# Linear attention and a mixture of adapters: numerators in four quarters of the array, slots in pairs of half-heads, no arithmetic on GpSimd

## The chip, the cores and the metric

The kernel runs on one core of a Trainium2 chip. The metric is device time in microseconds, the median of the runs given. Its engines are TensorE (PE, with the weight loads listed apart as PEld), VectorE (DVE), ScalarE (ACT), GpSimd (POOL) and SyncE (SP); each works through its own queue in order.

## What is computed

Two stages in a row. `B = H = 8`, sequence 576, head dimension 64; 4608 tokens of 512 features; 8 adapters of rank 16.

```python
q_p = phi(q, cos_w, sin_w)           # concat(relu(q)*cos(pos), relu(q)*sin(pos)): 128 features
k_p = phi(k, cos_w, sin_w)
kv  = einsum('bhsf,bhsd->bhfd', k_p, v)
z   = sum(k_p, axis=2)
num = einsum('bhsf,bhfd->bhsd', q_p, kv)
den = einsum('bhsf,bhf->bhs', q_p, z)[..., None] + 1e-06
x   = (num / den), heads side by side             # (4608, 512)
logits = x @ w_gate                               # 8 adapters, top 2, softmax over the two
out = x + sum over the two of weight * (x @ A[e]) @ B[e]
```

## The kernel before

**Tiling.** The batches go in four pairs `P` = 0 to 3 (batches 2P and 2P+1). A token index is `9*p + j`, so partition `p` (64 of them per batch) holds nine *slots* `j`; a slot of a pair is 128 tokens, one partition each. Heads come as four head pairs per batch, `2a + hh` with `a`, `hh` in 0, 1 (each head pair `c` has its two heads on the two halves of the partitions, `par`).

**Loads** (`load`, L437 and L439). K, V and Q of a batch are read as float32 and written as bfloat16 by DMAs that GpSimd issues, in halves (`a` = 0, then 1) for P = 0 and whole for P = 1 to 3: 12 half loads (288 KB written) and 18 whole ones (576 KB). The planner lets at most eight be in flight; a ninth waits for the first to land.

**KV stage of a batch.** `relu_k` (L446 on ACT, L448 on DVE or GpSimd) clips K in place. `vscale` makes VV, V scaled by cos and by sin of the position, one instruction per half on DVE (L464), nine per half, one for each slot, on ACT (L462) or on GpSimd (L458). `kv_mm` (L474) makes 72 products per batch, contraction 64, output 64 x 130, in 64 x 64 quarters of the array. `kv_evac` copies the sum from PSUM into BD, a block-diagonal tile (two heads on the diagonal, the rest zero, cleared once by `c_bd`, L364): two copies of 64 partitions for each KV result (L495 on ACT, L497 on DVE).

**A step of a slot.** `qt_mm` (L548) transposes Q by TensorE; `qt_evac` (L555, ACT) clips it into `qTcs[:,0]`; `qt_tan` (L562, DVE) multiplies by a table of tangents into `qTcs[:,1]` (the sine part is the cosine part times the tangent; the cosine cancels between numerator and denominator); `num_mm` (L574) forms 16 products of contraction 128, 64 columns of weights, 130 moving columns, against BD; `x_rden` (L587) and `x_xt` (L593) divide on DVE. P = 0 does a slot in two steps, one for each `a`; P = 1 to 3 in one.

**The adapters of two or three slots.** `xt_mm` (L603) transposes x, `xt_evac` copies it (a helper `copy`, L609 on ACT, L611 on DVE); `za_mm` (L622) multiplies by the adapters' A and the gate; `r_max`, `r_mask`, `r_sig`, `r_zg` (L637 to L661) choose the top two and weight them; `zg_mm` (L670) transposes; `dx_mm` (L681, L683) adds x and the adapters' B product; `osb` copies to SBUF; `store` (L694) is a DMA that SP issues. There are 13 such groups.

**Set-up.** `c_tan_mm` and `c_tan` make the table of tangents. `c_s4` fills S4, four shifted selections of the identity, on GpSimd (a memset, L352, and four copies, L354); `w_turn` (L403, L407) permutes A and the gate with it into AW, which every `za` needs.

**The order.** Nothing is ordered by hand in the text. Every step is given to a `Planner` with a duration, its needs, the buffers it uses and a due time; two long lists, `PLACES` (due times) and `CHOICE` (which of a step's engines), fix the outcome. The planner plays the steps through and the instructions are emitted in the order it finds, so each engine's queue, GpSimd's and SP's too, has a fixed order.

Of the kernel before, what the change touches and what calls it, by code (L numbers as in the profile page):

```python
# [14 lines left out]
ALU = mybir.AluOpType  # L15
# [4 lines left out]
LATENCY = {"PE": 0.22, "DVE": 0.15, "ACT": 0.18, "POOL": 0.2, "SP": 0.0}  # L20
DMA_RATE = 0.4e6
DMA_LATENCY = 1.4
# [6 lines left out]
    -101.8, -87.98, -82.42, -89.88, -75.22, -41.37, -75.2, -69.56, -114.61, -12.34, -86.45, -23.58, -23.54, -91.8,  # L29
    -45.05, -82.9, -23.77, -85.62, -30.55, -18.3, -22.53, -9.1, -38.95, -15.08, -65.11, -79.01, -56.96, -87.63,  # L30
    -56.28, 33.12, -45.48, 14.06, 72.95, -105.45, -131.87, -86.42, -70.75, -32.34, -16.92, -63.84, -25.14, -17,
    -43.98, -53.84, -48.45, -28.91, -9.38, -65.93, 17.22, -37.67, -38.2, -56.96, -43.01, -39.86, 30.02, 5.68, -111.22,
    -41.2, -64.86, -27.22, -29.22, -28.93, -4.21, -45.87, 23.7, -11.07, -12.97, 6.07, 70.31, -15.27, -0.79, 4.41,
    27.35, 80.46, 18.33, 55.75, -26.51, 7, 9.96, 5.54, 33.89, 26.46, 7.17, 53.85, -11.53, 34.73, 17.11, 14.52, 31.08,
    37.76, -22.01, -12.04, 32.65, -13.69, 63.75, 37.46, 47.44, 56.06, 90.6, -13.41, 25.03, 66.69, 7.86, 110.2, 48.71,
    70.14, 38.66, 102.11, 76.76, 2.02, 55.03, 13.27, 84.09, 49.59, -19.61, -52.1, -38.03, -36.37, -69.95, 12.85,
    -59.13, -37.48, -46.73, -48.82, -56.02, 13.89, 12.78, 15.65, -74.65, -22.83, -80.13, -60.11, 3.79, -21.31, -7.57,
    1.52, 3.72, -39.7, 0.51, 12.71, 28.08, -19.88, -4.04, 3.48, -28.4, -22.6, -107.17, -85.77, 16.75, 13.19, -35.9,
    -0.64, -30.78, 17.84, 81.24, 31.53, -2.77, 44.36, 65.3, 56.03, -1.94, 1.8, 32.86, 13.11, 4.12, 78.55, -26.18,
    28.07, 38.04, -31.26, 7.2, -32.61, -33.96, 31.37, -48.1, 23.76, 25.15, 68.01, 27.37, -44.65, 11.78, 45.25, 16.38,  # L40
    46.68, -22.64, 13.69, -25.72, -66.73, -0.53, -0.78, 71.43, 51.94, -23.6, -20.35, 24.46, 19.13, -1.34, 82.95,
    76.08, 23.7, -17.43, 12.4, -67.27, -50.55, -14.11, -46.79, 3.18, 15.81, -42.31, 39.03, 34.99, -39.11, 9.69, -18.7,
    -1.38, -56.98, 11.6, 73.43, 36.89, 10.81, 42.1, 9.54, -35.43, 6.89, 52.15, -23.59, 26.68, -12.27, 11.85, -7.33,
    25.43, -12.89, 48.12, -20.49, -5.27, -64.21, -51.87, 23.84, -27.03, -119.07, 63.64, 75.64, 28.22, -21.9, 39.45,
    76.49, 37.89, -23.87, 71.2, 66.21, 4.08, 64.69, 89.26, 43.11, 2.03, 58.06, 26.58, 65.92, 39.82, 30.03, 43.53,
    40.19, 71.59, 24.18, 64.92, 67.13, 22.92, -33.78, 25.67, 15.63, -6.52, 35.07, 11.11, 13.68, -24.37, 35.57, -39.99,
    -14.59, 78.65, -60.34, 46.82, 2.41, 16.29, -84.28, 12.65, -18.86, -31.15, -1.35, -75.63, -16.46, -81.15, -29.57,
    27.98, 47.97, 84.51, 85.87, 41.03, 66.04, 24.09, 50.35, -11.39, 79.39, 17.42, -26.65, 48.38, 31.89, 37.07, 11.76,
    19.75, -22.61, 31.8, -62.39, -30.12, -16.33, 78.09, 5.97, 40.99, 27.88, 53.62, 10.42, 32.04, 86.77, 43.98, 44.81,
    115.53, 53.53, 36.54, 45.14, 38.01, 72.24, 6.57, 97.39, 34.2, 67, -3.53, 18.47, 37.85, 94.56, 45.82, -9.21, 49.09,  # L50
    -29.83, -18.99, 63.72, -55.17, -7.86, 29.25, 43.71, 38.01, 53.05, 60.43, 30.63, 34.35, 40, 87.14, 3.29, 77.97, 52,
    51.6, 50.13, 10.4, 17.19, 59.75, 47.81, 17.21, 87.08, 61.73, 63.61, 93.31, 21.46, 55.47, 28.59, 31.38, -29.79,
    66.6, 49.37, -5.21, 0.73, 95.14, 89.51, 37.48, 19.5, 12.15, 80.24, 34.55, 53.72, 64.45, 4.15, 11.76, 57.62, 8.52,
    50.43, -6.44, -11.99, -14.41, -2.71, -20.63, 64.98, 69.49, 62.23, 41.36, -24.4, 64.99, -57.64, 32.08, 0.58, 0.18,
    -51.16, -19.52, -12.18, 37.93, 44.64, 53.74, 38.51, 16.7, 67.44, 60.26, 35.36, 55.27, 13.68, 23.18, -7.26, 30.35,
    2.86, 6.2, 51.01, 5.37, 37.66, 77.13, 79.47, 91.93, 14.78, 78.89, 35.85, 48.44, -3.31, -44.41, 67.02, 30.92,
    32.02, 42.36, -16.67, 44.14, 76.86, 65.68, -57.2, 42.99, 0.26, 95.71, -7.34, 49.33, 18.77, 68.25, 41.77, 57.26,
    73.06, 46.33, 58.36, 11.34, 119.4, 45.36, 152.93, -7.4, 79.07, 58.86, 28.26, 43.32, -37.77, 97.2, 15.02, 59.13,
    18.9, 55.86, 87.03, 74.35, 17.63, 89.53, 45.25, 75.81, -29.62, 68.21, 101.01, 86.91, 62, 92.26, 30.42, 20.38,
    89.46, 57.05, 38.98, 84.93, 88.33, 73.29, 10.34, 0.12, 86.89, 62.77, 41.35, 67.7, 72.99, 79.09, 20.79, 16.54,  # L60
    10.7, 23.33, 87.48, 88.63, 56.65, 13.55, 13.26, 70.38, 29.36, 90.47, 83.93, 74.51, 109.97, 81.76, 144.25, 15.07,
    68.55, 46.86, 113.6, 170.36, 66.36, 23.82, -21.97, 83.74, 94.21, 71.03, 89.76, 55.2, 84.29, 58.94, 49.33, 57.55,
    43.72, 58.13, 58.8, 75.42, 44.54, 72.47, 46.3, 17.6, 45.55, 112.71, 61.5, 49.18, 85.32, 91.99, 65.9, 49.76,
    102.45, 64.06, 109.11, 80.81, 98.13, 79.93, 109.32, 109.38, 106.64, 12.94, 78.35, 68.82, 51.61, 126.26, 51.11,
    48.51, 64.21, 89.64, 100.47, 96.74, 26.02, 67.7, 101.32, 95.25, 20.01, 35.48, 76.22, 70.63, 64.08, 8.78, 62.96,
    124.43, 72.7, 125.02, 67.06, 106.24, 98.77, 100.23, 116.59, 171.53, 99, 30.9, 96.57, 105.21, 70.96, 125.86, 61.23,
    98.87, 56.59, 37.62, 27.7, 95.05, 100.15, -77.12, 31.54, 170.49, 49.8, 58.28, 113.97, 78.54, 91.49, -30.01,
    113.81, 85.19, 124.99, 154.41, 102.88, 93.56, 84.87, 90.61, 132.83, 145.49, 116.13, 61.55, 20.49, 107.23, 74.22,
    92.66, 68.29, 175.11, 55.65, 161.84, 136.23, 34.27, 108.62, 44.45, 91.08,
]  # L70
CHOICE = [
    0, 0, 0, 0, 0, 0, 0, 0, 0, 0, 0, 0, 0, 0, 0, 0, 0, 0, 0, 0, 0, 0, 0, 0, 0, 0, 0, 0, 1, 0, 0, 1, 0, 0, 0, 0, 0, 0,
    1, 0, 1, 1, 0, 0, 0, 1, 0, 1, 0, 1, 1, 0, 0, 0, 1, 0, 0, 0, 0, 0, 0, 0, 0, 0, 1, 0, 0, 0, 1, 0, 0, 0, 0, 0, 2, 0,
    0, 0, 0, 0, 0, 1, 0, 1, 0, 0, 1, 0, 0, 0, 2, 0, 0, 0, 0, 0, 0, 0, 0, 0, 0, 1, 0, 0, 1, 0, 0, 0, 2, 0, 0, 0, 1, 0,
    0, 0, 0, 0, 0, 0, 0, 0, 0, 0, 0, 0, 0, 0, 0, 0, 0, 0, 0, 0, 0, 0, 0, 0, 0, 0, 0, 0, 0, 0, 0, 0, 0, 0, 0, 0, 0, 0,
    0, 0, 0, 1, 0, 0, 0, 0, 0, 0, 1, 0, 0, 0, 0, 0, 1, 0, 0, 0, 0, 0, 0, 0, 0, 0, 0, 0, 0, 0, 0, 0, 0, 0, 0, 0, 0, 0,
    0, 0, 0, 0, 0, 0, 0, 1, 0, 0, 0, 0, 0, 0, 0, 0, 0, 0, 0, 0, 0, 0, 0, 0, 0, 0, 0, 0, 0, 0, 0, 0, 1, 0, 0, 0, 0, 0,
    0, 0, 0, 0, 0, 0, 0, 0, 0, 0, 0, 1, 0, 0, 0, 0, 0, 0, 0, 0, 0, 0, 0, 0, 0, 0, 0, 0, 0, 0, 0, 0, 0, 0, 0, 0, 0, 0,
    0, 1, 0, 0, 0, 0, 0, 0, 0, 0, 0, 0, 0, 0, 0, 0, 0, 0, 0, 0, 0, 0, 0, 0, 0, 0, 0, 0, 0, 0, 0, 0, 0, 0, 0, 0, 0, 0,
    0, 0, 0, 0, 0, 0, 0, 0, 0, 0, 0, 0, 0, 0, 0, 0, 0, 0, 0, 0, 0, 0, 0, 0, 0, 0, 0, 0, 0, 0, 0, 0, 0, 0, 0, 0, 0, 0,  # L80
    0, 1, 0, 0, 0, 0, 0, 0, 0, 0, 0, 0, 0, 0, 0, 0, 0, 0, 0, 0, 0, 0, 0, 0, 0, 0, 0, 0, 0, 0, 0, 0, 0, 0, 0, 0, 0, 0,
    0, 0, 0, 0, 0, 0, 0, 0, 0, 0, 1, 0, 1, 0, 0, 0, 0, 0, 0, 0, 0, 0, 0, 0, 0, 0, 0, 0, 0, 0, 0, 0, 0, 0, 0, 0, 0, 0,
    0, 1, 0, 0, 0, 0, 0, 0, 1, 0, 0, 0, 0, 0, 0, 0, 0, 0, 0, 0, 0, 0, 0, 0, 0, 0, 0, 0, 0, 0, 0, 1, 0, 0, 0, 0, 0, 0,
    0, 0, 0, 0, 0, 0, 0, 0, 0, 0, 0, 0, 0, 0, 1, 0, 0, 0, 0, 0, 0, 0, 0, 0, 0, 0, 0, 0, 0, 0, 0, 0, 0, 0, 0, 0, 0, 0,
    0, 0, 0, 0, 0, 0, 0, 0, 0, 0, 0, 0, 0, 0, 0, 0, 0, 0, 0, 0, 0, 0, 0, 0, 0, 0, 0, 0, 0, 0, 0, 1, 0, 0, 0, 0, 0, 0,
    0, 1, 0, 0, 0, 0, 0, 0, 0, 0, 0, 0, 0, 0, 0, 0, 0, 0, 0, 0, 0, 0, 0, 0, 0, 0, 0, 0, 0, 0, 0, 0, 0, 0, 0, 0, 0, 0,
    0, 0, 0, 0, 0, 0, 0, 0, 1, 0, 1, 0, 0, 0, 0, 0, 0, 0, 0, 0, 0, 0, 0, 0, 0, 0, 0, 0, 0, 0, 0, 0, 0, 0, 0, 0, 0, 0,
    1, 0, 0, 1, 1, 0, 0, 0, 1, 0, 0, 0, 0, 0, 0, 0, 0, 1, 0, 0, 0, 0, 0, 0, 1, 0, 0, 1, 1, 0,
]

# [128 lines left out]
def kernel(  # L222
# [16 lines left out]
    ER = E * R  # L239
    AW_W = ER + E  # L240
    J = 9
    NP = S // J
    assert NP == 64 and H == 8 and D == 64 and B == 8 and DM == 512 and ER == 128
    W = D + 1
    VW = 2 * (D + 2)
    HALF_B = 128 * 2 * J * D * 4
    ALL = range(4)

    persist = ctx.enter_context(tc.tile_pool(name="persist", bufs=1))
    psum = ctx.enter_context(tc.tile_pool(name="psum", bufs=1, space=bass.MemoryType.PSUM))  # L250

# [99 lines left out]
    def c_s4():  # L351
        nc.gpsimd.memset(S4, 0.0)  # L352
        for i in range(4):
            nc.gpsimd.tensor_copy(S4[:, i].rearrange("p (q f) -> p q f", f=4)[:, :, i], ident)  # L354
# [455 lines left out]
```

## Time and profile before

| | |
|---|---|
| median of 8 runs | 131.61 us (130.78 to 132.88) |
| the profiled execution's own time | 132.88 us |
| its span, first to last instruction | 131.1 us |
| mean granted TensorE clock | 0.91 |
| DVE busy | 108.84 us in 300 instructions |
| PE busy, PE weight loads | 96.24 us, 72.39 us |
| ACT busy | 88.15 us in 200 instructions |
| POOL busy | 51.78 us in 57 instructions |
| DMA bytes | 24.14 MB: 14.43 MB by the loads' queue, 9.44 MB by the stores' |

The span is 1.8 us shorter than the time of its own execution and 0.5 us below the median. "Busy" counts the time in which an engine has at least one instruction at work; two neighbours on DVE can overlap by about 0.1 us, so durations sum to more than busy time. A matmul's end is modelled and has some 0.2 us of pipeline in it, so eight matmuls of 0.22 us each take far less than eight times that. In the rows by slices, a digit is the busy share of 1/40 of the span (3.28 us) in tenths.

### The profile page before, as it was taken

Reading aid. Unit: us, or ns where it says so; the run is one execution under the profiler, and the core shown is the slowest. Engines: PE = TensorE matmul, PEld = TensorE weight load, DVE = VectorE, ACT = ScalarE, POOL = GpSimd, SP = SyncE. Lnnn points to the kernel's source line nnn. Section 1 sums busy time; section 2 is a strip of 40 time slices with the busy share of each in tenths; the row PEclk is TensorE's granted clock in tenths of the full one; section 3 lists DMA queues with packets and bytes.
Section 4 is the critical chain, followed back from the end, with each engine's and each line's share of the span. In section 5 each row is a group of like instructions: output and inputs, shape, how many; then the busy total and the mean of one; then the engine's idle time right before and its main releaser. Section 6 shows DMA issues by size and latency. Waiting matters only on the chain.

```text
span 131.1 us, 4453 instructions
## 1 busy us (share of the span) xinstructions
PE 96.2 (73%) x1860; PEld 72.4 (55%) x1872; DVE 108.8 (83%) x300; ACT 88.2 (67%) x200; POOL 51.8 (39%) x57
## 2 busy tenths in 40 slices
PE   0153494896999874863999995367989999999830
PEld 0122482795876363723886772256866768786400
DVE  6634798789979894999889799999999899998940
ACT  3954699569963897990647797177544887877440
POOL 6996984228429999399000059300000000000000
PEclk9999998559999999996589999778699999999995
DMA  1999999999999999999999999900000655005583
GB/s 12 157 148 205 207 207 205 208 192 208 210 206 209 207 324 324 210 208 207 208 208 324 209 237 295 294 26 7 0 5 2 243 242 241 4 12 232 240 345 138
DMA packets 15989, 24.14 MB, mean 184 GB/s; under 512 B 1889, under 2 KB 14305, under 8 KB 15969
## 3 DMA queue, kind: packets, MB, share of 16 engines
q0 software_dynamic: 14096, 14.43, 66.5%
q1 hardware_dynamic: 1872, 9.44, 17.9%
q8 instruction: 14, 0.23, 0.7%
q14 instruction: 7, 0.05, 0.1%
HBM read 28.85 MB, written 9.44 MB: 292 GB/s over the span
## 4 chain that ended last, share of the span: by engine, by line
PE 32%; DVE 31%; ACT 12%; POOL 9%; issue 6%; DMA 6%; POOLq 0%; DVEq 0%; ACTq 0%
DVE qTcs L562 9%; PE pnd L574 9%; ACT VV L462 7%; POOL VV L458 7%; DVE xt L593 6%; PE pnd L474 6%; DMA Kr<-in_k_dram 6%; PE ps L622 5%; PE ps L603 4%; PE ps L548 4%; DVE zg L661 3%; PE ps L681 2%; DVE rden L587 2%; DVE osb L611 2%; DVE m L637 2%
## 5 line engine op out<-in xcount | busy, mean ns | idle before, releaser
L574 PE MATMUL pnd<-BD,qTcs 128*64 128x130 bf16 x576 | 28.7, 244 | 8.6 <-DVE qTcs L562 3.3
L574 PEld LDWEIGHTS <-qTcs 128*64 128x64 bf16 x576 | 22.0, 122 | 13.7 <-issue 6.8
L593 DVE TENSOR_TENSOR xt<-pnd,rden 128x512 bf16<-128x512 f32 (+1 forms) x45 | 25.8, 582 | 1.1
L562 DVE TENSOR_TENSOR qTcs<-qTcs,TT 128x512 bf16<-128x512 bf16 (+1 forms) x45 | 25.9, 598 | 0.4 <-ACT qTcs L555 0.2
L555 ACT ACTIVATE qTcs<-ps 128x512 bf16<-128x512 bf16 (+1 forms) x45 | 21.4, 511 | 5.2 <-PE ps L548 4.7
L609 ACT COPY xT<-ps 128x512 bf16<-128x512 bf16 x26 | 15.1, 583 | 13.7 <-PE ps L603 13.7
L462 ACT ACTIVATE VV<-Vb,TVf 128x128 bf16<-128x128 bf16 (+1 forms) x54 | 19.3, 443 | 3.7 <-DMA Vb<-in_v_dram 3.7
L448 POOL TENSOR_SCALAR Kr<-Kr 128x2304 bf16<-128x2304 bf16 x2 | 12.5, 6244 | 16.6 <-DMA Kr<-in_k_dram 16.6
L609 ACT COPY osb<-ps 128x512 f32<-128x512 f32 (+1 forms) x31 | 16.5, 561 | 3.3 <-PE ps L683 1.6
L474 PE MATMUL pnd<-VV,Kr 64*64 64x130 bf16 x576 | 13.5, 256 | 7.0 <-DVE Kr L448 3.1
L603 PE MATMUL ps<-ident,xt 128*128 128x128 bf16 x144 | 14.1, 228 | 6.1 <-DVE xt L593 5.5
L474 PEld LDWEIGHTS <-Kr 64*64 64x64 bf16 x576 | 11.7, 131 | 8.6 <-DVE Kr L448 3.4
L464 DVE TENSOR_TENSOR VV<-Vb,TV 128x2304 bf16<-128x2304 bf16 (+1 forms) x13 | 14.6, 1143 | 1.2 <-DMA Vb<-in_v_dram 1.2
L548 PE MATMUL ps<-ident,Qb 128*64 128x128 bf16 x288 | 15.0, 247 | 0.1
L603 PEld LDWEIGHTS <-xt 128*128 128x128 bf16 x144 | 9.2, 100 | 10.2 <-DVE xt L593 6.8
L681 PE MATMUL ps<-xt,ident 128*128 128x512 bf16 x34 | 13.0, 382 | 0.6 <-DVE osb L611 0.3
L548 PEld LDWEIGHTS <-Qb 128*64 128x64 bf16 x288 | 11.3, 128 | 3.0 <-issue 1.8
L622 PE MATMUL ps<-AW,xT 128*128 128x136 bf16 x144 | 11.6, 234 | 0.1
L458 POOL TENSOR_SCALAR VV<-Vb,TVf 128x256 bf16<-128x256 bf16 x9 | 10.1, 1132 | 2.2 <-DVE xT L611 2.2
L622 PEld LDWEIGHTS <-xT 128*128 128x128 bf16 x144 | 9.8, 103 | 1.2 <-issue 0.2
L683 PE MATMUL ps<-Ball,zgT 128*128 128x512 bf16 x26 | 9.9, 380 | 0.6 <-DVE zgT L611 0.3
L495 ACT CAST BD<-pnd 64x520 bf16<-64x520 f32 (+1 forms) x11 | 5.9, 538 | 4.9 <-PE pnd L474 3.9
(62 smaller groups left out, 119.4 us busy)
## 6 DMA issues: line engine op xcount, KB each, us to landing
out_dram<-osb SPq DMA_DIRECT2D x11, 768.0 KB, 4.4
Kr<-in_k_dram POOLq DMA_DIRECT2D x6, 576.0 KB, 19.3
Vb<-in_v_dram POOLq DMA_DIRECT2D x6, 576.0 KB, 16.3
Qb<-in_q_dram POOLq DMA_DIRECT2D x6, 576.0 KB, 21.9
Vb<-in_v_dram POOLq DMA_DIRECT2D x4, 288.0 KB, 8.1
Kr<-in_k_dram POOLq DMA_DIRECT2D x4, 288.0 KB, 8.1
Qb<-in_q_dram POOLq DMA_DIRECT2D x4, 288.0 KB, 9.2
out_dram<-osb SPq DMA_DIRECT2D x1, 512.0 KB, 3.3
```

Source lines behind the costliest of these rows:

```text
L458: nc.gpsimd.tensor_scalar(out=o[:, :, j], in0=i[:, :, j], scalar1=TVf[:, cs, j:j + 1], scalar2=None, op0=ALU.mult)
L462: nc.scalar.activation(o[:, :, j], i[:, :, j], AF.Copy, scale=TVf[:, cs, j:j + 1])
L474: nc.tensor.matmul(out=pt[64 * hh:64 * hh + 64, par, a * 2 * W:(a + 1) * 2 * W], lhsT=kt[64 * par:64 * par + 64, 2 * a + hh, j, :], rhs=vt ...
L548: nc.tensor.transpose(out=pt[64 * hh:64 * hh + 64, o:o + 128], in_=qt[:, 2 * a + hh, j, :], identity=ident)
L555: nc.scalar.activation(tQT[S_(uqt)][:, 0, 0:n].rearrange("p g s -> p (g s)"), pB(up)[:, 0:n * 64], AF.Relu)
L562: nc.vector.tensor_tensor(out=t[:, 1, 0:n], in0=t[:, 0, 0:n], in1=TT[:, j].unsqueeze(1).to_broadcast([128, n, NP]), op=ALU.mult)
L574: nc.tensor.matmul(out=nd[64 * b2:64 * b2 + 64, a, 0:4 * W].rearrange("p (h e w) -> p h e w", h=2, e=2)[:, :, par], lhsT=qt[:, cs, (b2 * l ...
L593: nc.vector.tensor_tensor(out=tXT[S_(uxt)].rearrange("p (a h d) -> p a h d", a=2, h=4)[:, aa[0]:aa[-1] + 1], in0=nd_view(und, aa)[:, :, :, ...
L603: nc.tensor.transpose(out=pB(up)[:, c * 128:(c + 1) * 128], in_=tXT[S_(uxt)][:, c * 128:(c + 1) * 128], identity=ident)
L609: nc.scalar.copy(o, i)
L622: nc.tensor.matmul(out=pF(uza)[:, n * AW_W:(n + 1) * AW_W], lhsT=tXTT[S_(u)][:, c, :], rhs=AW[:, c, :], start=(c == 0), stop=(c == 3))
L681: nc.tensor.matmul(out=pF(udx), lhsT=ident, rhs=tXT[S_(uxt)], start=True, stop=False)
```

## The change

1. `num_mm` no longer uses a block-diagonal tile. `kv_evac` is one copy of 128 partitions into a plain tile KVs; each numerator product is cut in two, contraction 64 and 65 moving columns: 32 products a step where there were 16, in the four quarters of the array (two row halves `hh`, two column halves `b2`), each row half with a PSUM bank of its own. The tile BD and its four memsets go.
2. P = 0 and P = 1 (`SPLIT`) form steps of two neighbouring slots and one `a`, instead of (P = 0) one slot and one `a` or (P = 1) one slot and both. P = 1's K, V and Q are loaded in halves too: 24 half loads and 12 whole ones. The tile xt now holds two slots; there are 11 of them (before, 12 of one slot).
3. GpSimd's alternatives for `relu_k` and `vscale` are removed. In the order before, GpSimd did two whole relu's of K and one whole half of VV. GpSimd keeps the loads and the set-up.
4. `c_s4` is a memset and one `affine_select` of 128 x 2048. The tangent and weight set-ups are cut into parts that each hold one PSUM bank.
5. The planner's constants and durations are changed a little and both lists are new, so the order on every engine is another.

```diff
-        nc.gpsimd.memset(S4, 0.0)
-        for i in range(4):
-            nc.gpsimd.tensor_copy(S4[:, i].rearrange("p (q f) -> p q f", f=4)[:, :, i], ident)
+        nc.gpsimd.memset(S4, 0.0)
+        nc.gpsimd.affine_select(out=S4, in_=S4, compare_op=ALU.not_equal, fill=1.0, base=0,
+                                pattern=[[1, 4], [-1, DM]], channel_multiplier=4)
...
-                (nc.gpsimd if eng == "POOL" else nc.vector).tensor_scalar(out=t, in0=t, scalar1=0.0, scalar2=None, op0=ALU.max)
+                nc.vector.tensor_scalar(out=t, in0=t, scalar1=0.0, scalar2=None, op0=ALU.max)
...
-            if eng == "POOL":
-                for j in range(J):
-                    nc.gpsimd.tensor_scalar(out=o[:, :, j], in0=i[:, :, j], scalar1=TVf[:, cs, j:j + 1],
-                                            scalar2=None, op0=ALU.mult)
-            elif eng == "ACT":
+            if eng == "ACT":
...
-    def kv_evac(hh, aa, up, ubd, eng):
-            o = tBD[S_(ubd)][64 * hh:64 * hh + 64, :, lo:lo + n, :, 66 * hh:66 * hh + W]
-            i = pND[S_(up)][64 * hh:64 * hh + 64, :, lo * 2 * W:(lo + n) * 2 * W]
+    def kv_evac(aa, up, ukv, eng):
+            o = tKV[S_(ukv)][:, :, lo:lo + n, 0:W]
+            i = pND[S_(up)][:, :, lo * W:(lo + n) * W].rearrange("p e (x w) -> p e x w", w=W)
...
-                        for b2 in range(2):
-                            bd = tBD[S_(("BD", 2 * P + b2))]
-                            nc.tensor.matmul(
-                                out=nd[64 * b2:64 * b2 + 64, a, 0:4 * W].rearrange(
-                                    "p (h e w) -> p h e w", h=2, e=2)[:, :, par],
-                                lhsT=qt[:, cs, (b2 * len(aa) + n) * 2 + par, :],
-                                rhs=bd[:, par, a, cs].rearrange("p (h w) -> p h w", h=2)[:, :, 0:W],
-                                start=(cs == 0), stop=(cs == 1), skip_group_check=True)
+                        for hh in range(2):
+                            for b2 in range(2):
+                                kv = tKV[S_(("KV", 2 * P + b2))]
+                                nc.tensor.matmul(
+                                    out=nd[64 * b2:64 * b2 + 64, hh, (2 * x + par) * W:(2 * x + par + 1) * W],
+                                    lhsT=qt[64 * hh:64 * hh + 64, cs, ((jj * 2 + b2) * na + n) * 2 + par, :],
+                                    rhs=kv[64 * hh:64 * hh + 64, par, 2 * aa[n] + cs, 0:W],
+                                    start=(cs == 0), stop=(cs == 1), skip_group_check=True)
...
+        if P in SPLIT:
+            parts = [(js, [a]) for a in range(2) for js in ([0, 1], [2, 3], [4, 5], [6, 7], [8])]
+        else:
+            parts = [([j], [0, 1]) for j in range(J)]
```

The instruction counts that follow from the two orders, with the shapes of the profile:

| | before | after |
|---|---|---|
| PE num products | 576 of 128 x 64, 130 columns | 1152 of 64 x 64, 65 columns |
| DVE tangent, reciprocal, xt | 27 full + 18 half each | 34 full + 4 half each |
| DVE VV | 8 whole, 5 half | 7 whole, 13 half |
| DVE relu of K | 3 whole, 2 half | 3 whole, 6 half |
| DVE KV copies; BD memsets | 4 of 520, 5 of 260, on 64 partitions; 4 | 4 of 260, on 128; none |
| DVE copies xT, osb (512), osb (256), zgT | 10, 6, 2, 5 | 8, 6, 3, 4 |
| ACT VV | 27 of 256, 27 of 128 | 9 of 256, 27 of 128 |
| ACT KV copies; xT | 8 of 520, 3 of 260, on 64 partitions; 26 | 4 of 520, 4 of 260, on 128; 28 |
| POOL relu of K, VV | 2, 9 | none |
| the last four loads issued | V7, K7, Q6, Q7 (the digit is the batch) | Q6, Q7, K7, V7 |

## The prediction

> **What bounds the kernel now.** I read the page first: busy time by engine, then the rows by slices.
>
> ```profile
> PE 96.2 (73%) x1860; PEld 72.4 (55%) x1872; DVE 108.8 (83%) x300; ACT 88.2 (67%) x200; POOL 51.8 (39%) x57
> ...
> DVE  6634798789979894999889799999999899998940
> ...
> POOL 6996984228429999399000059300000000000000
> ...
> DMA  1999999999999999999999999900000655005583
> GB/s 12 157 148 205 207 207 205 208 192 208 210 206 209 207 324 324 210 208 207 208 208 324 209 237 295 294 26 7 0 5 2 243 242 241 4 12 232 240 345 138
> ```
>
> DVE is the fullest and runs at 9 from slice 16 to nearly the end. The loads saturate the DMA engines until slice 26, 86 us; for the 43 us after that, everything is on chip. So two things could set the end: DVE's total, and the arrival of the last load plus what must follow it. Next, the groups of DVE and POOL by shape: is 108.8 us work?
>
> ```profile
> L562 DVE TENSOR_TENSOR qTcs<-qTcs,TT 128x512 bf16<-128x512 bf16 x27 | 21.3, 807 | 0.3 <-ACT qTcs L555 0.2
> L464 DVE TENSOR_TENSOR VV<-Vb,TV 128x2304 bf16<-128x2304 bf16 x8 | 10.9, 1387 | 0.0
> L448 POOL TENSOR_SCALAR Kr<-Kr 128x2304 bf16<-128x2304 bf16 x2 | 12.5, 6244 | 16.6 <-DMA Kr<-in_k_dram 16.6
> ```
>
> The tangent multiply has a mean of 807 ns, but its median (by tile, both shapes) is 414 and its longest 5789. DVE's and POOL's instructions in order of time show where:
>
> ```profile
> 54.78 6.03 POOL L448 TENSOR_SCALAR Kr<-Kr 128x2304 bf16<-128x2304 bf16 x1 [2.15 <-DMA Kr<-in_k_dram]
> 55.19 5.79 DVE L562 TENSOR_TENSOR qTcs<-qTcs,TT 128x512 bf16<-128x512 bf16 x2
> 61.04 0.98 PE L574 MATMUL pnd<-BD,qTcs 128*64 128x130 bf16 x14 [3.30 <-DVE qTcs L562]
> 62.65 0.58 ACT L609 COPY xT<-ps 128x512 bf16<-128x512 bf16 x1 [3.73 <-PE ps L603]
> ```
> ```profile
> 76.78 6.46 POOL L448 TENSOR_SCALAR Kr<-Kr 128x2304 bf16<-128x2304 bf16 x1 [14.44 <-DMA Kr<-in_k_dram]
> ```
> ```profile
> 77.28 5.79 DVE L562 TENSOR_TENSOR qTcs<-qTcs,TT 128x512 bf16<-128x512 bf16 x1
> ```
>
> Both times a tangent multiply that starts inside a relu on GpSimd ends just as that relu ends (55.19+5.79 = 60.98 against 60.81; 83.07 against 83.24). DVE counts as busy while it stands still, and PE and ACT then wait for it. The chain that ended last runs through both:
>
> ```profile
> 55.28 5.72 DVE qTcs L562 x2
> ...
> 77.37 5.71 DVE qTcs L562
> ```
>
> **The change, part by part.** The sum is made on the span, 131.1 us.
>
> *GpSimd's arithmetic goes.* Unblocked, two tangents take 0.75 us and one 0.41 (rows at 71.32 and 75.68), so the stalls are 5.79-0.75 = 5.04 and 5.79-0.41 = 5.38: -10.4 us of DVE, all on the chain. What is late next is DVE itself, which has work waiting at both places. GpSimd's 22.6 us of arithmetic becomes work of DVE or ACT, counted next.
>
> *DVE's work recounted*, by means without stalls. Tangents, 27 at 0.41 + 18 at 0.28 = 16.1, become 34 and 4: 15.1 (-1.0). Reciprocal and xt, 27 at 0.88 + 18 at 0.60 = 34.6, become 32.4 (-2.2). KV copies 4.9, now 4 at 0.42 (-3.2; 128 partitions instead of 64 should cost nothing). BD memsets -2.0. Copies xT, osb, zgT -0.5. VV 14.6 becomes 13 at 0.75 + 7 at 1.35 = 19.2 (+4.6). Relu of K +1.8 (four more halves at 0.46). Sum -2.5; neighbours overlap, busy time is about 0.9 of summed durations, so -2.3 us. The new xt writes two runs of 256; the nearest row, 0.69 us, is kept (0.05 either way on 16 steps is 0.8 us).
>
> *Set-up on GpSimd.* Before, the S4 memset (12.60 to 14.42) held a relu of K on DVE from 13.07 to 14.74: 1.67 instead of 0.46, 1.2 us on the chain. After, memset and affine_select follow the Ball load, the fifteenth DMA, which waits for the seventh to land: about 16 us, just where five tangents stand in DVE's queue, with the first num, reciprocal and xt behind them. No row shows DVE against affine_select. The Trainium skill, "SBUF — State Buffer", section "SBUF: two separate sides", says that the pair of ports that DVE and GpSimd share is an exclusive lock for the whole instruction, and the relu rows agree; by that rule affine_select blocks too. Its length lies between the identity's, 0.29 us (128 x 128), and sixteen times that, 4.7. So the loss is from 0 (it falls between) to 1.8+4.7 = 6.5; as the memset before cost two thirds of its length, I take 3.2, 2.0 more than before. The loads queued behind on POOL are covered by the eight in flight, some 1.4 us each. Six more load issues at 0.74 us cost nothing: POOL then only waits for landings. w_turn needs S4, but the first za ran at 35.9.
>
> *ACT* loses 18 VV instructions (-7.4), about 2 of KV copies, gains two xT (+1.2): near 80 us. It binds nowhere, so 0.
>
> *PE.* Num products double. Here a rule of the Trainium skill speaks against the change: "TensorEngine Tiling (Array Packing)", section "Instruction Overhead", gives each matmul some 60 cycles whatever its size; "TensorE: Matmul & The Clock Gate", section "Back-to-back issue gap", makes that about 25 ns for 1 to 64 columns. By it a full step is 32 x 25 = 0.80 us. The trace's own quarters:
>
> ```profile
> 54.69 1.25 PE L474 MATMUL pnd<-VV,Kr 64*64 64x130 bf16 x72
> ```
> ```profile
> 109.82 0.64 PE L574 MATMUL pnd<-BD,qTcs 128*64 128x130 bf16 x16
> ```
>
> 72 quarter products with their weight loads take 1.25 us, of which 0.22 is the last one's pipeline: 14.3 ns a pair, below the 25. A num step is 0.47 us without its tail (109.82 to the next group at 110.29), 29 ns a product. At 14.3 ns a pair the new step is 0.46, the same; if half the columns halve it, 0.23. Bounds -0.24 to +0.33 us a step; I take 0, because weight loads do not shrink with the columns. PE then ends near its old 96 us.
>
> *Waits.* A slot's transpose now needs both a-steps of its pair of slots; in P = 0 it already waited for a = 1, in P = 1 the halves land one by one, earlier than a whole. K7 and V7 are now the last loads; behind V7's two VV instructions on DVE stand 21 us of work (11 reciprocal-xt pairs at 0.75 is 8.2, nine tangents 3.3, five adapter groups 6.3, copies 3.2).
>
> *Sum.* 131.1 - 10.4 - 2.3 + 2.0 = 120.4 with DVE's idle time as before (22.3). Of that, 10.2 us lay between 8.8 and 88 us (the busy times by stage); 0.9 of it was KV copies of DVE waiting for ACT's half, which is gone, and another 1 I give to the half loads of P = 1: 118.5. A second way, from the arrival: loads alone move at 207 GB/s, 14.43/0.207 = 69.7 us; a 0.79 MB store in a slice of 324 GB/s takes about 2.0; with a 4 us start and six or seven stores before V7, it lands at 86.7 or 88.7. Then 2.6 of VV, 21 of DVE, 2 of idle (before: 3.2 us after the last VV), 4.2 from DVE's last instruction to the end (126.9 to 131.1): 116.5 to 118.5. I take a span of 117.5. The median stood 0.5 above the span: **118.0 us**. The profiled execution, if it stands 1.8 above its span again, would show 119.3.
>
> **The rivals.**
> *Arrival binds (20%).* K7 landed at 76.8 before, with only the Qs behind; now K7 and V7 come last, and the more stores get ahead, the later: at ten stores V7 lands at 94.7, and relu, VV, KV, copy and the whole of P = 3 follow. End 94.7+2.6+21+2+4.2 = 124.5; with eight or nine stores 122. For it: DMA at 9 throughout. Against it: DVE can hardly have finished ten groups by then.
> *PE gains (14%).* At 0.23 us a step PE loses 36 x 0.24 = 8.6 us of 96; from 88 to 120 us it is as full as DVE (29.6 of 32 against 29.8), so half would be seen: 118 - 4 = 114. For it: pairs at 14 ns match 130 columns shared by four. Against it: twice the weight loads.
> *The issue floor binds, slower (4%).* If a quarter pair takes over 25 ns, PE gains 0.33 us on 36 steps, 12 us, and it is the fuller engine wherever num runs. That eats the whole gain of 13; from about 26 ns the kernel is slower. If weight load and product each pay 25, a step is 1.6 us, +40, and PE ends near 150. Against it: the 14.3 measured in the same shape.
> *It does not do what it says (2%).* If the load issues themselves held DVE like the relu did, the stalls would come back as many small ones: 36 x 0.3 = 11, hence 131. Against it: in the trace three tangents beside a load issue at 26.20 take 0.69 us, no more than elsewhere.
>
> **How the numbers follow.** The sum, 60%: 118. Arrival 20%, 122 to 124. PE gains 14%, 114. Slower 4%, same 2%. Leaving out a tenth at each end gives 113.5 to 123.5. Faster by over 0.5% (what a measurement here can tell from no change) 0.94, within 0.5% 0.02, slower 0.04.
>
> **What would show it.** Right: no tangent over 1 us after 25 us; DVE busy near 97 us; num steps at about 0.46; the last VV on DVE near 91; a long DVE instruction near 16 to 21 us beside S4. Wrong: V7 landing after 92; num steps over 0.7; DVE idle beyond 24 us, since the new order may wait where the old had a backlog.

## The result, and the profile after

The changed kernel takes 129.49 us (median of 11 runs, 127.91 to 131.59), the kernel before 131.58 beside it: a ratio of 0.981, interval 0.978 to 0.984. Ratios, here and below, leave out the runs that were over 1.5% longer than the fastest of their kernel, so they are not quite those of the medians. It is faster by some 2 us where 13.6 were forecast. The profiled execution took 129.28 us, with a span of 127.5 and a granted clock of 0.92.

The page of the changed kernel, busy times, rows by slices (3.19 us each) and the instruction queue:

```profile
PE 92.3 (72%) x2437; PEld 67.8 (53%) x2448; DVE 95.3 (75%) x279; ACT 79.7 (63%) x174; POOL 33.2 (26%) x49
...
DVE  0543797958683899998994479439999999998850
...
DMA  1999999999999999999999999913303491006683
...
q8 instruction: 19, 0.31, 1.0%
```

DVE lost 13.5 us of busy time, near the 12.7 that were reckoned. But the span fell by 3.6: DVE now stands idle for 127.5-95.3 = 32.2 us, where it was idle for 22.3. The row shows where, counting slices from 0: gaps in slices 6 to 12 and 21 to 26, nearly all of them while the loads run, and 8s and 9s from slice 27 on until the end nears. By stages (start:end, length, then busy time of PE, PEld, DVE, ACT, POOL, granted clock, DMA share, GB/s), the changed kernel from 20 to 88 us:

```profile
20.00:88.00 68.00, 51.87 (x1419) 39.27 (x1418) 51.76 (x140) 42.12 (x93) 17.44 (x24) 0.85 1.11 213
```

and the kernel before:

```profile
20.00:88.00 68.00, 52.62 (x1085) 40.67 (x1088) 60.81 (x146) 48.28 (x108) 34.81 (x27) 0.87 1.15 226
```

DVE is busy for 9 us less in the same 68, yet it did not get further: 140 instructions instead of 146. (Of the 60.81 before, some 10.4 were the two stalls beside GpSimd's relus, which count as busy.) The groups of DVE in the changed kernel say that the stalls are gone, and what came instead:

```profile
L545 DVE TENSOR_TENSOR qTcs<-qTcs,TT 128x512 bf16<-128x512 bf16 x34 | 13.2, 419 | 4.8 <-ACT qTcs L539 4.8
```

Here a full tangent takes 419 ns in the mean (before, 807). Idle time before them grew from 0.3 us to 4.8; they wait for ACT, and ACT for the transposes of PE. PE's instructions in order of time, in the middle of that stretch (the bracket is PE's idle time before the row, and what ended it):

```profile
65.82 0.36 PE L468 MATMUL pnd<-VV,Kr 64*64 64x130 bf16 x10 [0.37 <-DVE xt L585]
68.71 1.29 PE L468 MATMUL pnd<-VV,Kr 64*64 64x130 bf16 x62 [2.53 <-issue]
...
75.38 0.45 PE L560 MATMUL pnd<-KVs,qTcs 64*64 64x65 bf16 x32
75.76 0.64 PE L532 MATMUL ps<-ident,Qb 128*64 128x128 bf16 x16
...
77.96 0.23 PE L665 MATMUL ps<-ident,zg 128*128 128x128 bf16 x1
80.55 0.37 PE L665 MATMUL ps<-ident,zg 128*128 128x128 bf16 x2 [2.36 <-issue]
```

PE stops in the middle of a group whose data are all there: 10 products of one KV result, 2.5 us of nothing, then the other 62. What ends the pause is "issue", nothing that the trace of data shows. Such pauses stand at 21.0, 27.0, 32.9, 38.8, 68.7 and 80.6 us, and the count of weight loads at the pauses (222, 350, 478, 606, then 1246, 1502) differs by 128 or a multiple: 128 pairs of a weight load and a product, 256 instructions of PE. Together the six pauses take 11 us. The raw records of the instruction queue (q8, 16384 bytes a packet, 64 bytes for each of 256 instructions) start at:

```
before: 19.0 28.6 35.6 41.5 50.9 57.2 66.1 72.1 79.0 91.1 96.6 101.7 108.8 115.1
after:  18.7 24.7 30.6 36.6 42.5 48.3 54.3 60.2 66.4 72.3 78.3 83.2 88.6 92.8 97.3 103.7 107.8 111.5 117.4
```

In the changed kernel one packet follows another every 5.8 to 6.2 us, without a break, until 78.3 us; the loads end at 84.4. In the kernel before most distances are longer. Two distances tie the packets to PE. At each of the six pauses PE goes on 2.3 us after the start of a packet (21.0 after 18.7, 27.0 after 24.7, and so on). And in both kernels, as long as the loads run, the next packet starts 2.2 to 3.9 us after PE's first weight load of a block: it looks as if a block is asked for when PE enters the one before it. The two together, 3.6 and 2.3 us at the pauses, are the 5.9 us of a full turn. A block whose work takes longer hides this turn, a shorter one shows it.

The chain that ended last has the same name in it. Changed kernel, then the kernel before:

```profile
DVE 37%; PE 33%; issue 14%; DMA 6%; ACT 4%; POOL 3%; POOLq 0%; DVEq 0%; ACTq 0%
```
```profile
PE 32%; DVE 31%; ACT 12%; POOL 9%; issue 6%; DMA 6%; POOLq 0%; DVEq 0%; ACTq 0%
```

**Theory.** PE's instructions come from memory, 256 at a time, one block each 5.9 us at best as long as the loads fill the DMA engines. That is 46 ns a product, however short the product is. The change took PE from 3744 to 4896 instructions (twice the weight loads of the trace; the expectations have 4 fewer), and from 20 to 88 us it lives on that supply: 1419 products at 5.92/128 us are 65.6 of the 68 us (before, 1085: 50.2). DVE waits for ACT and PE, and PE for its instructions. **Rivals:** the new order itself, which may wait where the old had a backlog; the quarter products or the plain copy, by a cost of their own; a fixed price for each product at any time.

### The profile page after: what moved, and what is told of

It is laid out like the page before. It is cut to its first block, busy times and chain, and to the rows that moved or that the text cites. A ratio compares the mean times of both kernels' runs of the same rounds, so it can differ in the third digit from the quotient of the medians.

```text
span 127.5 us, 5551 instructions
## 1 busy us (share of the span) xinstructions
PE 92.3 (72%) x2437; PEld 67.8 (53%) x2448; DVE 95.3 (75%) x279; ACT 79.7 (63%) x174; POOL 33.2 (26%) x49
## 4 chain that ended last, share of the span: by engine, by line
DVE 37%; PE 33%; issue 14%; DMA 6%; ACT 4%; POOL 3%; POOLq 0%; DVEq 0%; ACTq 0%
DVE xt L585 11%; PE pnd L468 7%; DMA Vb<-in_v_dram 6%; DVE qTcs L545 5%; PE pnd L560 5%; PE ps L532 5%; DVE VV L458 5%; PE ps L599 4%; PE ps L676 4%; DVE zg L656 3%; PE ps L678 3%; DVE rden L572 2%; PE ps L617 2%; DVE osb L606 2%; DVE m L632 2%
## 5 line engine op out<-in xcount | busy, mean ns | idle before, releaser
L539 ACT ACTIVATE qTcs<-ps 128x512 bf16<-128x512 bf16 (+1 forms) x38 | 20.2, 572 | 11.2 <-PE ps L532 10.8
L560 PE MATMUL pnd<-KVs,qTcs 64*64 64x65 bf16 x1152 | 18.4, 205 | 4.6 <-DVE xt L585 3.0
L560 PEld LDWEIGHTS <-qTcs 64*64 64x64 bf16 x1152 | 14.4, 116 | 10.4 <-issue 7.4
L458 DVE TENSOR_TENSOR VV<-Vb,TV 128x1152 bf16<-128x1152 bf16 (+1 forms) x20 | 18.6, 961 | 1.7 <-DMA Vb<-in_v_dram 1.7
L532 PEld LDWEIGHTS <-Qb 128*64 128x64 bf16 x288 | 11.4, 133 | 14.5 <-DMA Qb<-in_q_dram 9.3
L545 DVE TENSOR_TENSOR qTcs<-qTcs,TT 128x512 bf16<-128x512 bf16 (+1 forms) x38 | 14.1, 405 | 4.8 <-ACT qTcs L539 4.8
L676 PE MATMUL ps<-xt,ident 128*128 128x512 bf16 x36 | 15.0, 421 | 1.1 <-DVE osb L606 0.3
L456 ACT ACTIVATE VV<-Vb,TVf 128x128 bf16<-128x128 bf16 (+1 forms) x36 | 11.8, 415 | 1.6 <-DMA Vb<-in_v_dram 1.6
L572 DVE RECIPROCAL rden<-pnd 128x8 f32<-128x8 f32 (+1 forms) x38 | 7.4, 197 | 3.9 <-PE pnd L560 3.9
L446 DVE TENSOR_SCALAR Kr<-Kr 128x1152 bf16<-128x1152 bf16 (+1 forms) x9 | 6.0, 671 | 2.5 <-DMA Kr<-in_k_dram 2.5
L483 ACT CAST KVs<-pnd 128x260 bf16<-128x260 f32 (+1 forms) x8 | 3.9, 487 | 5.8 <-PE pnd L468 5.8
```

Source lines behind the costliest of these rows:

```text
L458: nc.vector.tensor_tensor(out=o, in0=i, in1=TV[:, cs].unsqueeze(1).to_broadcast([128, n, J, D]), op=ALU.mult)
L532: nc.tensor.transpose(out=pt[64 * hh:64 * hh + 64, o:o + 128], in_=qt[:, 2 * a + hh, j, :], identity=ident)
L539: nc.scalar.activation(tQT[S_(uqt)][:, 0, 0:n].rearrange("p g s -> p (g s)"), pB(up)[:, 0:n * 64], AF.Relu)
L545: nc.vector.tensor_tensor(out=t[:, 1], in0=t[:, 0], op=ALU.mult, in1=TT[:, js[0]:js[-1] + 1].unsqueeze(2).to_broadcast([128, len(js), n // ...
L560: nc.tensor.matmul(out=nd[64 * b2:64 * b2 + 64, hh, (2 * x + par) * W:(2 * x + par + 1) * W], lhsT=qt[64 * hh:64 * hh + 64, cs, ((jj * 2 + ...
L676: nc.tensor.matmul(out=pF(udx), lhsT=ident, rhs=xt_view(P, j, uxt), start=True, stop=False)
```

## The experiments

| | edit | median us | ratio to before | PE instructions | DVE busy, idle |
|---|---|---|---|---|---|
| e1_after_16 | changed order, 16 products | 125.04 | 0.940 [0.929, 0.952] | 3744 | 99.5, 22.1 |
| e8_after_16_again | the same | 124.13 | 0.941 [0.936, 0.946] | 3744 | 99.6, 22.2 |
| e9_after_16_cut | e1, products cut | 130.17 | 0.981 [0.974, 0.988] | 4896 | 99.9, 29.0 |
| e10_after_again | the changed kernel | 128.38 | 0.973 [0.965, 0.980] | 4896 | 95.0, 30.6 |
| e5_mixed | e1, P = 3 as changed | 124.50 | 0.943 [0.939, 0.947] | 4032 | 99.3, 22.9 |
| e2_before_nopool | before, no GpSimd arithmetic | 125.06 | 0.946 [0.938, 0.955] | 3744 | 100.8, 22.9 |
| e3_before_cut | before, products cut | 134.55 | 1.019 [1.010, 1.027] | 4896 | 101.2, 31.8 |
| e6_nopool_cut | both | 134.50 | 1.023 [1.016, 1.030] | 4896 | 101.2, 30.3 |

Busy and idle are those of the profiled execution, idle being its span less its busy time; in e9_after_16_cut that execution took 130.63 us.

**The doubled products taken back: e1_after_16 and e8_after_16_again.** The changed kernel with BD, its memsets and 64-partition copies again; the order of every step stays the changed one.

```diff
-                        for hh in range(2):
-                            for b2 in range(2):
-                                kv = tKV[S_(("KV", 2 * P + b2))]
-                                nc.tensor.matmul(out=nd[64 * b2:64 * b2 + 64, hh, (2 * x + par) * W:(2 * x + par + 1) * W], ...
+                        for b2 in range(2):
+                            bd = tBD[S_(("KV", 2 * P + b2))]
+                            nc.tensor.matmul(out=nd[64 * b2:64 * b2 + 64, x, 0:4 * W].rearrange(
+                                "p (h e w) -> p h e w", h=2, e=2)[:, :, par], ...
```

> The changed kernel with its own order, but the numerators again as 16 products a step against a block-diagonal KV tile (two copies instead of one for each KV result, the four memsets in DVE's idle start): 3740 PE instructions instead of 4892, no arithmetic on GpSimd. Theory F (PE is starved of instructions: they come in packets of 16 KB, 256 instructions, and while the loads fill the DMA engines one packet takes 5.9 us): 14 packets instead of 19, the pauses of 1 to 2.5 us in the middle of PE's groups go, 119 to 123 us in spite of about 2 us more of copies. Rival O (the new order itself waits, or its last loads come too late): 127 to 131 us, since order and loads are the same.

> The same kernel as e1_after_16, run beside e5_mixed on one chip so that the two can be compared: 124 to 126, as there.

125.04 and 124.13, with 4.2 us more work on DVE than the changed kernel has. DVE's idle time is 22.1 and 22.2 us, what the kernel before had. The same stretch as above, in e8_after_16_again:

```profile
20.00:88.00 68.00, 55.95 (x1265) 42.48 (x1265) 61.26 (x173) 50.45 (x112) 18.51 (x25) 0.95 1.15 225
```

From 20 to 88 us DVE does 173 instructions, where the changed kernel does 140: in the same order, so it is not the order that waits. The expectation was still missed, by 1 to 2 us: the theory had allowed 123 at most. Its range fits the spans, 121.6 and 121.8, which stand 1.7 us below the times of their executions.

**The kernel before without GpSimd's arithmetic: e2_before_nopool.**

```diff
-                (nc.gpsimd if eng == "POOL" else nc.vector).tensor_scalar(out=t, in0=t, scalar1=0.0, scalar2=None, op0=ALU.max)
+                nc.vector.tensor_scalar(out=t, in0=t, scalar1=0.0, scalar2=None, op0=ALU.max)
...
-            if eng == "POOL":
-                for j in range(J):
-                    nc.gpsimd.tensor_scalar(out=o[:, :, j], in0=i[:, :, j], scalar1=TVf[:, cs, j:j + 1],
-                                            scalar2=None, op0=ALU.mult)
```

> The kernel before with its order unchanged, but the two relus of K and the half of VV that GpSimd did run on DVE at the same places of the order. The prediction's first step: 10.4 us of stalls go, 2.9 us of work come (2 x 0.75 + 1.35): 123 to 125 us. Theory F agrees, at most 1 or 2 us more, because with 3740 PE instructions the packets come more seldom than one in 5.9 us most of the time. Rival (the stalls were covered by the loads' arrival, so that taking them away gives little): 129 us or more.

125.06, beside 131.34 for the kernel before: this one edit is worth 5.4% [4.5, 6.2], more than the whole change. DVE takes over two relus at 0.75 and one VV instruction at 1.35, so 10.4 - 2.85 = 7.6 us should go from its busy time; 8.0 went (108.8 to 100.8), and 7.4 of the span. No tangent stalls any more:

```profile
L558 DVE TENSOR_TENSOR qTcs<-qTcs,TT 128x512 bf16<-128x512 bf16 x27 | 10.7, 414 | 0.3 <-ACT qTcs L551 0.2
```

The stall step of the prediction holds.

**The products cut in the kernel before: e3_before_cut.** The same columns in twice as many products, with BD and contraction 128.

```diff
-                    for cs in range(2):
-                        for b2 in range(2):
-                            bd = tBD[S_(("BD", 2 * P + b2))]
-                            ...
-                                rhs=bd[:, par, a, cs].rearrange("p (h w) -> p h w", h=2)[:, :, 0:W],
+                    for h in range(2):
+                        for cs in range(2):
+                            for b2 in range(2):
+                                bd = tBD[S_(("BD", 2 * P + b2))]
+                                ...
+                                    rhs=bd[:, par, a, cs, 66 * h:66 * h + W],
```

> The kernel before, GpSimd's arithmetic included, with each numerator product of 130 columns cut in two of 65, contraction 128 as it was: the same columns through the array, but 1152 PE instructions more, 4892 in all. Theory F: 19 packets; nine came by 79 us, at 31 per cent more instructions some three more are needed by then at 5.9 us each, partly hidden by DVE's stalls: 133 to 138 us. Rival (what slows the changed kernel is its quarters, their drains or its order, not the count of instructions): 131 to 132.5 us.

134.55, 1.9% slower, with DVE's idle time at 31.8: the starvation comes without quarters, plain copy or new order. But DVE's busy time fell from 108.8 to 101.2. GpSimd still did its two relus, at 53.01 and 77.50, but with everything late mostly other DVE instructions stood beside them:

```profile
L562 DVE TENSOR_TENSOR qTcs<-qTcs,TT 128x512 bf16<-128x512 bf16 x27 | 13.7, 519 | 0.4 <-ACT qTcs L555 0.3
```

The same 27 tangents as before, at 519 ns instead of 807: 7.6 us less. One still stalls, for 3.24 us at 80.10. Part of the price of the count is paid from there, and it is greater than the 1.9% shows.

**The two together: e6_nopool_cut**, the diffs of e2_before_nopool and of e3_before_cut in one kernel.

> The kernel before with GpSimd's relus and VV given to DVE, as in e2_before_nopool, and each numerator product cut into two of 65 columns, as in e3_before_cut: both in the order of the kernel before. Supply theory: without the stalls the queue of TensorE is drained faster, so 1152 more TensorE instructions ahead of the last load cost more than the 3.2 us they cost in e3_before_cut: 129 to 131.5. Rival, a small fixed price for each product: the two edits add up, 125.1 + 3.2 = 128.3 or less.

134.50, above both expectations. The edit that was worth 6.3 us with 16 products is worth nothing with 32 (134.55 without it). One reason is DVE's busy time, 101.2 us in both: in e3_before_cut most of the stalls had gone already, and what was left of them is about as long as the work that comes back from GpSimd. The other is the instruction packets, which start at:

```
e3_before_cut: 18.0 25.4 31.4 37.7 43.6 53.5 59.4 65.4 71.7 77.5 82.8
e6_nopool_cut: 18.3 25.5 31.5 37.5 43.5 54.5 60.5 66.4 72.6 78.5 83.1
```

Packet by packet they stand within 1.1 us of each other. From 25 to 43.5 us and from 54 us until the loads end they come about 6 us apart; the 10 us between are one block that both kernels work on for longer, with waits for ACT among its work. I had priced the count as an addend to a kernel that kept its stalls. The price itself is seen between e2_before_nopool and this kernel, which differ only in the count: from 0.946 to 1.023, some 10 us. In e3_before_cut most of it was hidden.

**The same cut in the changed order: e9_after_16_cut, beside the changed kernel, e10_after_again.** The edit is that of e3_before_cut, made to e1_after_16.

> The kernel of e1_after_16 (the changed order, block-diagonal tile, DVE's copies and memsets with it), each numerator product cut into two of 65 columns with contraction 128: as many TensorE instructions as the changed kernel, but no quarter products and no plain copy. If it is the count of instructions that the changed kernel pays for, this one loses what e1_after_16 had gained, and is above the changed kernel by its extra copies on DVE: 129 to 133. If it is the quarter products or the plain copy with its order that cost, it stays near e1_after_16: 124 to 126.

> The changed kernel unaltered, beside e9_after_16_cut on one chip: 129 to 130, as before.

130.17 and 128.38; the ratio went from 0.941 [0.936, 0.946] with 16 products to 0.981 [0.974, 0.988] with 32. Order, tile and DVE's work are those of e1_after_16, and the columns are the same, only in twice as many products: so it is the count, and not the quarters. The array itself is hardly slower: a step takes 0.54 us (76.73 to 77.27), and 0.49 with 16 products (72.64 to 73.13 in e8_after_16_again). PE's pauses are back at the same places:

```profile
39.87 0.36 PE L541 MATMUL ps<-ident,Qb 128*64 128x128 bf16 x6 [1.96 <-issue]
...
69.98 1.94 PE L470 MATMUL pnd<-VV,Kr 64*64 64x130 bf16 x62 [2.27 <-issue]
81.83 0.27 PE L669 MATMUL ps<-ident,zg 128*128 128x128 bf16 x2 [2.10 <-issue]
```

The repeat of the changed kernel was 0.6 us below the low end of its expectation and inside the spread of its 11 runs.

**Doubled only late: e5_mixed.** In e1_after_16, P = 3 alone uses the plain copy and 32 quarter products.

```diff
+            pl.add("num", one("PE", 0.48 * h + 0.12, (num_mm_q if P == 3 else num_mm)(P, nj, aa, uqt, und)), ...
```

> The changed kernel with its order; P = 0 to 2 form numerators by 16 products against the block-diagonal tile as in e1_after_16, P = 3 by 32 quarter products against the plain copy. P = 3's numerators run after the loads have landed. If the supply of TensorE's instructions is what the doubled count costs, and it costs mainly while the loads fill the DMA engines, doubling it in the last nine slots alone costs little: within 1.5 us of e1_after_16, and less by the halves of KV copies saved late, so 123 to 126. If the doubled count costs the same wherever it stands (a fixed price for each product), a quarter of what lies between e1_after_16 and the changed kernel comes back: 126 to 127.5.

124.50, beside 124.13 for all 16: 288 more instructions, all after the loads have landed (86.1 us; the first of them runs at 97.1), cost 0.4 us, less than the spread of either kernel's runs. A price for each product at any time would have given 126 to 127.5. The saving on DVE by the plain copy cannot be seen either (99.3 against 99.6).

**The supply by itself: e4_stream.** 3000 quarter pairs of 65 columns that wait for nothing, beside the loads.

```diff
+        for i in range(PAIRS):
+            hh, b2 = (i // 2) % 2, i % 2
+            nc.tensor.matmul(out=pnd[64 * b2:64 * b2 + 64, hh, 0:65], lhsT=wt[64 * hh:64 * hh + 64, :],
+                             rhs=mv[64 * hh:64 * hh + 64, :], start=True, stop=True, skip_group_check=True)
```

> No attention and no adapters: the K, V and Q of all batches are loaded and not used, PE makes 3000 independent quarter products of 65 columns (6000 instructions) from two constant tiles, then a constant is stored. Theory F: while the loads run, packets of PE instructions are 5.9 us apart and PE pauses every 128 products; after the last load they are 3 us apart or less, and PE runs at 7 to 15 ns a pair. Rival (an issue floor of some 25 ns a product): 128 products in 3.2 us, with loads or without.

```profile
1.07 3.29 PE L52 MATMUL pnd<-mv,wt 64*64 64x65 bf16 x223 [1.07 <-DVE mv L43]
7.14 1.97 PE L52 MATMUL pnd<-mv,wt 64*64 64x65 bf16 x128 [2.78 <-issue]
13.06 1.98 PE L52 MATMUL pnd<-mv,wt 64*64 64x65 bf16 x128 [3.95 <-issue]
...
86.92 1.98 PE L52 MATMUL pnd<-mv,wt 64*64 64x65 bf16 x128 [1.48 <-issue]
```

223 pairs are there at the start. Then blocks of exactly 128 come every 5.92 us, and run in 1.98, of which 0.22 is the last one's pipeline: 13.8 ns a pair. PE stands for two thirds of the time. After the loads have landed a block comes every 3.45 to 3.73 us (the last after 4.0), where 3 or less was expected, and PE still pauses at each.

**Which products it meets: e7_stream_wide.** 640 full products, then 640 of 64 weight columns and 130 moving ones.

```diff
+        for i in range(640):
+            nc.tensor.matmul(out=pnd[:, i % 2, 0:128], lhsT=wt, rhs=mv[:, 0:128], start=True, stop=True)
+        for i in range(640):
+            b2 = i % 2
+            nc.tensor.matmul(out=pnd[64 * b2:64 * b2 + 64, (i // 2) % 2, 0:130], lhsT=wt[:, 0:64], rhs=mv, ...
```

> Leaves the whole computation out and stores a constant: beside the loads alone, TensorE gets 640 products of 128 x 128 weights and 128 columns, then 640 of 128 x 64 weights and 130 columns, one after the other, waiting for nothing. Supply theory (128 products in 5.9 us beside loads, 3.5 us without): the first kind needs about 53 ns each by the rows of TensorE, 6.8 us for 128, so it runs without a pause, 34 us for 640; the second, 29 ns each or 3.7 us for 128, pauses about 2.2 us in each block beside the loads and hardly at all after them. Rival, that the pauses of e4_stream belong to products in quarters of the array: no pauses in either kind, 640 of the second in 19 us.

```profile
1.20 37.21 PE L51 MATMUL pnd<-mv,wt 128*128 128x128 bf16 x640 [1.20 <-DVE mv L43]
38.33 6.58 PE L54 MATMUL pnd<-mv,wt 128*64 128x130 bf16 x223
47.02 3.82 PE L54 MATMUL pnd<-mv,wt 128*64 128x130 bf16 x128 [2.10 <-issue]
52.94 3.82 PE L54 MATMUL pnd<-mv,wt 128*64 128x130 bf16 x128 [2.10 <-issue]
```

The full ones take 58 ns each, 7.4 us for 128, and never pause: slower than the supply, they hide it. The others, 29 ns each, run out after 223, and then pause 2.10 us in every 5.92. So the pauses need no quarters. They need products that are faster than the supply: 29 ns pause, 58 do not, and 46 is the limit that 5.92 us for 128 gives.

## Why the prediction was wrong

- *GpSimd's arithmetic goes, -10.4*: right as to the stalls (no long tangent is left, mean 419 ns). Alone, in e2_before_nopool, it took 7.4 us from the span: 8.0 of DVE's busy time (the 10.4, less 2.85 of work that came back to DVE and was booked apart, would be 7.6), less 0.6 that its idle time grew.
- *DVE's work recounted*: right. Busy 95.3 us, "near 97" forecast. ACT 79.7, "near 80".
- *Set-up on GpSimd, +2.0*: too high by about 2.2. Only the memset held DVE: the relu of K at 16.45 took 1.50 us instead of 0.46, 1.0 us in all, where 3.2 were reckoned and 1.2 had been lost before. The rule that the prediction used (the Trainium skill, "SBUF — State Buffer", section "SBUF: two separate sides") names only some of DVE's instructions, those in a two-port mode or with two operands in SBUF; the prediction left this out when it took `affine_select` to block whatever DVE did. Those that ran beside it took their usual 0.69 and 0.20 us.
- *PE, "I take 0"*: **this step failed.** It costed a product by its time on the array, and that was nearly right: a step now takes 0.38 us (the group at 75.38 to the next at 75.76), less than the 0.46 taken. But it left out that each product is two instructions that must first arrive. The kernel before used 1085 of the 68/5.92 x 128 = 1470 products that the supply allows at most between 20 and 88 us; the changed kernel got 1419 of them through and paused for more. From 9 to 88 us DVE is idle for 19.8 us, where it was for 10.2, and for 11.4 in e8_after_16_again.
- *Sum, "with DVE's idle time as before (22.3)", less 2*: the term in which the failure appears. It measured 32.2. DVE's 95.3 with the idle time of e8_after_16_again, 22.2, would be the span of 117.5 that was taken. That is arithmetic with two kernels' numbers, not a run.
- *Arrival*: the loads ended at 84.4 us (84.3 before), earlier than the 86.7 to 88.7 forecast, so the arrival rival falls. Four stores went ahead of the last load, not six or seven; and the forecast's own terms, 4 + 69.7 us and 2.0 for each store, make 85.7 to 87.7. V7's VV still ran late, at 97.4 instead of 91: DVE had no pause of over 0.2 us between 85.7 and 97.4, it was behind with the work ahead of it.
- *Of the rivals*, the issue floor was refuted as put: the pair takes 12 to 14 ns, not 25. The rule that it leaned on, 60 cycles for each matmul (the Trainium skill, "TensorEngine Tiling (Array Packing)", section "Instruction Overhead"), would have given 0.80 us a step; the trace has 0.38. A price for each product there is, but in the supply, and only where products outrun it. "PE gains" had its faster step, and nothing of it reached the end.
- The prediction named the sign itself, "DVE idle beyond 24 us", but put it down to the order. The page of before gave no clear hint: its 6.8 us of "issue" before the weight loads of num, and 6% of the chain, are 6.3 us and 5% in e8_after_16_again, which loses little to the supply. What could have been reckoned is the number of packets: 14 before, 19 for 4896 instructions.

The Trainium skill, "Runtime: NRT & Kernel Launch", section "Instruction fetch mechanics", says that instructions are refilled in blocks of 16 KiB, 256 instructions, and that the cost of crossing a block is mostly hidden. The blocks agree with the runs here. "Mostly hidden" held for the kernel before, and not for 4896 instructions beside saturating loads: 1.0 to 2.5 us show at each of six boundaries.

**What stays open.** Why a block takes 5.92 us beside the loads was not tried. A packet is under way for some 1.0 us, and PE goes on 2.3 us after its start; the 3.6 us before its start, which shrink to 0.8 to 1.5 once the loads of the changed kernel have landed, are unexplained. PE's granted clock from 66 to 88 us was 0.77 in the profiled execution of the changed kernel and 1.00 in e1_after_16; in the repeat e10_after_again it was 0.92 there, and DVE was idle for 30.6 us all the same, so the clock is not the main cause. Its share in the spread of 127.3 to 131.6 us was not told apart.

## What to carry to other kernels

Count TensorE's instructions, two for each product with its weights, against what can arrive while loads saturate the DMA engines: here 256 per 5.9 us. While that supply binds, a split into smaller products saves nothing where they are shorter than 46 ns each. Its price can hide behind a stall that stood in the same place: 1.9% in e3_before_cut, some 8% once the stalls were gone. In a profile it shows as "issue" pauses inside groups of matmuls at equal counts; the best kernels here undo the split and keep the rest (124.1 to 125.0 us).

## What was not expected of the hardware

- The supply: 5.92 us for 256 instructions beside loads at some 207 GB/s, 3.45 to 3.73 without them, 223 products in stock at the start of a stream.
- A quarter pair of 65 columns costs 12 to 13.8 ns, one of 130 columns 14.3 in the kernel before: in quarters the columns hardly count. With contraction 128 they do: 0.54/32 us = 17 ns for 65 columns in e9_after_16_cut, 0.49/16 us = 31 ns for 130 in e8_after_16_again.
- The `affine_select` of 128 x 2048 on GpSimd took 2.01 us, and DVE ran beside it as if it were not there:

```profile
17.71 2.01 POOL L355 TENSOR_SCALAR_AFFINE_SELECT S<-S 128x2048 bf16<-128x2048 bf16 x1
```
```profile
18.10 0.69 DVE L585 TENSOR_TENSOR xt<-pnd,rden 128x512 bf16<-128x512 f32 x1
18.70 0.20 DVE L572 RECIPROCAL rden<-pnd 128x8 f32<-128x8 f32 x1
18.94 0.69 DVE L585 TENSOR_TENSOR xt<-pnd,rden 128x512 bf16<-128x512 f32 x1
```

These DVE instructions read their large operand from PSUM. The memset before it did hold a relu that reads and writes SBUF alone:

```profile
15.81 1.82 POOL L354 MEMSET S<- 128x2048 bf16 x1
```
```profile
16.45 1.50 DVE L446 TENSOR_SCALAR Kr<-Kr 128x1152 bf16<-128x1152 bf16 x1
```

That the place of the operand makes the difference is a guess: no run here tried the same instruction both ways.
